# The first batch's V loaded in runs of three keys and ordered by TensorE, with w_in behind it in one go

## The chip, the cores and the metric

The kernel runs on one core of a Trainium2 chip. A core has TensorE (PE) for matrix products, VectorE (DVE), ScalarE (ACT) and GpSimd (POOL) for work on rows, and SyncE (SP), which here issues the DMAs. PSUM is where TensorE writes; SBUF is where everything else lies. The metric is the device time of one execution in microseconds, taken as the median of several runs.

## The reference

Inputs are q, k and v of 8 batches, 8 heads, 576 positions and 64 values each, and two weights, w_in (512 x 2048) and w_out (2048 x 512), with two scalars s and b. What is computed:

```
scores = q @ k^T / 8, kept where |i - j| <= 32       (per batch and head)
attn   = softmax(scores) @ v
x      = attn, heads side by side: 4608 tokens x 512
h      = relu(x @ w_in)
out    = (s * h * h + b) @ w_out                      (4608 x 512, float32)
```

All inputs are float32; the kernel casts them to bf16 for the products.

## The kernel before, in words

The whole program is a list of tasks. A task has an engine, one or more instructions, an estimated cost, the buffers that it reads and writes, and a key that says how early it is wanted. A planner inside the program (`plan`) walks through the tasks with a model of engines and DMA queue and writes down an order for each engine; `emit` then puts waits on semaphores between the engines. A change of one task's cost or key can therefore move instructions anywhere, and on each engine the order is then fixed: an instruction that waits holds up all behind it.

Attention of a batch is cut into tiles of 64 positions (nine of them) and units of two tiles (five, the last with one tile). The first batch goes its own way at the start. q and k come in pairs of heads, `load_pair`, nine positions to a partition in runs of 2304 bytes; they are cast (line 592 or 593), turned by TensorE against an identity (line 599) into W, which is two PSUM banks, and copied out (lines 605 and 606). The scores of one head pair (line 832) go to SC or O, two more pairs of banks, and ScalarE takes the exponential (line 854).

V of a unit comes with one DMA (`load_v`, line 566): keys on partitions, heads and values side by side, so that each run in memory has the 64 values of one key and head, 256 bytes. It is cast to bf16 by GpSimd or VectorE (`cast_v`, line 575) straight into VB, where it stands with its keys in order. The attention products (line 747) read VB and the exponentials; unit u needs V of units u and u-1. They go to SC, O or AVN. VectorE divides by the row sums (lines 769 and 771), TensorE turns the result (line 778) and ScalarE copies it to XT (line 786).

The second part works on token blocks of 96, 128, 128, 160, 256, 256 and then 512 tokens. `s1` multiplies XT with w_in into one of the two W banks (line 980), ScalarE applies relu (987), VectorE squares (989) into GT. `s2` multiplies GT with w_out into O (998), and line 1014 scales and adds before the store. For the first four blocks the w_out product is split into `early` (line 1029), which follows the arrival of w_out. w_in and w_out come in eight pieces of 512 KB each through a ring of eight staging buffers (line 538) and are all cast by GpSimd (line 541); a piece is issued when GpSimd or another engine has freed its buffer. The column sums of w_out (line 1038) need all of w_out.

The order of SP's loads is fixed by rising keys: the eight pairs of q and k, then what `ORDER0` says, numbers below 8 for units of V and 8 to 11 for the four quarters of w_in:

```
ORDER0 = (0, 1, 8, 2, 3, 4, 9, 10, 11)
EV0 = ("pool", "dve", "pool", "dve", "pool")
```

then the two scalars, w_out, and q, k and V of the second batch. `EV0` names the engines that cast the units of V. GpSimd also makes the masks of the later batches (lines 470, 475, 505, 508), some of them between casts of weights.

Of the kernel before, what the change touches and what calls it, by code (L numbers as in the profile page):

```python
# [12 lines left out]
D = 64  # L13
# [11 lines left out]
LAG = 1  # L25
K0 = ("dve", "dve", "dve", "dve")
Q0 = ("act", "pool", "pool", "pool")
ORDER0 = (0, 1, 8, 2, 3, 4, 9, 10, 11)
WINE = ("pool", "pool", "pool", "pool")
FIRST = ((0, 0), (1, 0), (2, 0), (0, 1), (1, 1), (2, 1), (3, 0), (3, 1), (0, 2), (1, 2), (2, 2), (3, 2), (0, 3), (1, 3), (2, 3), (3, 3))  # L30
WOUTE = (("pool", "pool"),) * 4
# [9 lines left out]
CASTE = (("pool", "pool"), ("pool", "dve"))  # L41
SLACK = (1000.0, 2000.0, 3000.0, 3000.0)
PACEV = ((-1,-1,0,0,1),(0,0,1,1,2),(0,0,1,1,2))
EV0 = ("pool", "dve", "pool", "dve", "pool")
BANK1 = ("W", "SC", "SC", "AVN", "AVN")
EV1 = ("pool", "pool", "pool", "pool", "pool")
EV2 = ("dve",) * 5
# [269 lines left out]
def bass_sliding_window_symmetric__then__act_starrelu_kernel(  # L317
# [23 lines left out]
    with ExitStack() as es:  # L341
# [45 lines left out]
        ONESW = sb((128, 128), BF16, "onesw")  # L387
        IDENT = sb((128, 128), BF16, "ident")
        GT = [sb((128, 16, 512), BF16, "gt") for _ in range(2)]
        R1 = [sb((128, 512), BF16, "r1") for _ in range(NR1)]  # L390
        OUTS = [sb((128, DM), F32, "outs") for _ in range(NOUT)]
        CVEC = sb((128, DM), F32, "cvec")
# [134 lines left out]
        def load_weights(which, i, x, key, eng):  # L527

            si = take("stg", NSTG)
            stg = STG[si].rearrange("p (a c) -> p a c", a=2)  # L530
            if which == "in":
                src = moe_w_in.rearrange("(kc p) f -> p kc f", p=128)[:, 2 * x:2 * x + 2, i * 512:(i + 1) * 512]
                dst = WIN_BF[:, 2 * x:2 * x + 2, i * 512:(i + 1) * 512]
            else:
                f0 = 4 * i + 2 * x
                src = moe_w_out.rearrange("(fc p) c -> p fc c", p=128)[:, f0:f0 + 2, :]
                dst = WOUT_BF[:, f0:f0 + 2, :]
            add("sp", lambda e: e.dma_start(stg, src), 600.0, writes=[("STG", si)], key=key,
                dma=("l", 16, 100.0 if which == "in" else 85.0))
# [32 lines left out]
        def cast_v(c, u, key, eng, slack):  # L572
            vs, vb, n = number(c, u) % NUNIT, number(c, u) % (2 * NUNIT), 64 * len(tiles(c, u))
            add(eng, (lambda e: e.copy(VB[0:n, vb, :, 0:D], VST[0:n, vs, :, :])) if eng == "act" else
                (lambda e: e.tensor_copy(VB[0:n, vb, :, 0:D], VST[0:n, vs, :, :])),  # L575
                {"act": 617.0, "dve": 420.0, "pool": 750.0}[eng],
                reads=[("VST", vs)], writes=[("V", vb)], key=key, slack=slack)

        def load_pair(b, name, pr, load_key):

# [310 lines left out]
        def attention():  # L891
            seq = {"k": -200.0}

            def nxt():
                seq["k"] += 1.0
                return seq["k"]
# [5 lines left out]
            for pr in range(NPAIR):  # L902
# [425 lines left out]
```

## Time and profile before

| | us |
|---|---|
| median of three timed runs | 318.2 (317.32 to 319.56) |
| profiled execution | 316.02 |
| its span, first to last instruction | 314.2 |
| TensorE busy in the span | 297.0 (95%) |
| VectorE, ScalarE, GpSimd busy | 190.1, 140.8, 89.3 |
| mean granted TensorE clock | 0.989 |

The busy time of TensorE counts an instruction from its start to its modelled end; matmuls overlap. The granted clock is the share of full speed that the chip lets TensorE run at. DMA shares above 1 come from overlapping packets. A line of the chain of waits gives the start in us from the span's start, the length and what it was.

### The profile page before, as it was taken

How to read it: one execution, taken by the hardware profiler on the slowest of the kernel's cores; microseconds unless marked ns; L12 is line 12 of the kernel's file. 1: busy time of each engine (PE TensorE's matmuls, PEld its weight loads, DVE VectorE, ACT ScalarE, POOL GpSimd, SP SyncE). 2: the span in 40 equal slices, each digit the busy share in tenths (PEclk: the TensorE clock that was granted, in tenths of full speed). 3: DMA queues.
4: the chain of work that ended last, by engine and by line, in shares of the span. 5: the costliest groups of instructions: out<-in, count | busy, mean ns of one | idle time of the engine just before them, and what ended most of it. 6: DMA issues, size and time to landing. Idle time of an engine off the chain costs nothing.

```text
span 314.2 us, 8417 instructions
## 1 busy us (share of the span) xinstructions
PE 297.0 (95%) x3557; PEld 162.3 (52%) x3602; DVE 190.1 (61%) x377; ACT 140.8 (45%) x219; POOL 89.3 (28%) x109
## 2 busy tenths in 40 slices
PE   7698999899999999999999999999999999999995
PEld 3477855477644554544444444444444444444444
DVE  3455594875796796887578477856555543333312
ACT  4736435266635775653266335444444333333300
POOL 3468864635136136132313421260000000000000
PEclk9969999999999999999999999999999999999999
DMA  7999999998998998798999799997111110100122
GB/s 261 296 303 392 388 286 282 191 172 263 254 166 210 288 160 163 237 228 140 219 297 165 161 190 336 166 157 176 52 52 50 52 46 33 37 35 33 37 96 74
DMA packets 98985, 56.13 MB, mean 179 GB/s; under 512 B 74048, under 2 KB 88128, under 8 KB 98944
## 3 DMA queue, kind: packets, MB, share of 16 engines
q1 hardware_dynamic: 98944, 55.56, 74.8%
q8 instruction: 29, 0.48, 0.7%
q14 instruction: 12, 0.10, 0.1%
HBM read 36.70 MB, written 9.44 MB: 147 GB/s over the span
## 4 chain that ended last, share of the span: by engine, by line
PE 79%; DMA 9%; DVE 4%; issue 3%; POOL 2%; ACT 2%; SPq 1%; POOLq 0%
PE w L980 34%; PE o L998 32%; DMA stg<-in_k_dram 4%; PE avn L747 3%; DMA stg<-in_moe_w_in_dram 3%; DMA vst<-in_v_dram 2%; PE o L1029 2%; PE avn L1029 2%; DVE gt L989 2%; PE sc L689 2%; PE w L599 1%; ACT r L987 1%; PE avn L778 1%; POOL win L541 1%; DVE outs L1014 1%
## 5 line engine op out<-in xcount | busy, mean ns | idle before, releaser
L980 PE MATMUL w<-xt,win 128*128 128x512 bf16 (+4 forms) x813 | 141.3, 315 | 3.6 <-issue 1.9
L987 ACT ACTIVATE r<-w 128x512 bf16<-128x512 f32 (+2 forms) x148 | 86.6, 586 | 107.2 <-PE w L980 88.8
L998 PE MATMUL o<-wout,gt 128*128 128x512 bf16 (+1 forms) x510 | 123.1, 372 | 2.0 <-issue 1.4
L989 DVE TENSOR_TENSOR gt<-r 128x512 bf16<-128x512 bf16 (+2 forms) x148 | 75.0, 511 | 79.3 <-ACT r L987 78.7
L980 PEld LDWEIGHTS w<-xt,win 128*128 128x128 bf16 x832 | 70.2, 99 | 53.8 <-issue 0.8
L998 PEld LDWEIGHTS o<-wout,gt 128*128 128x128 bf16 x528 | 50.5, 98 | 54.6
L638 POOL CAST nat<-stg 128x1024 bf16<-128x1024 f32 (+1 forms) x21 | 24.6, 1174 | 62.1 <-DMA stg<-in_q_dram 41.3
L655 POOL COPY kt<-ktr 128x512 bf16<-128x512 bf16 (+1 forms) x30 | 30.8, 1027 | 38.4 <-DMA ktr<-nat 36.9
L717 ACT ACTIVATE ex<-sc 128x1024 bf16<-128x1024 f32 (+1 forms) x29 | 29.7, 1023 | 22.2 <-PE avn L747 21.3
L1014 DVE SCALAR_TENSOR_TENSOR outs<-o,sb,cvec 128x512 f32<-128x512 f32 (+1 forms) x35 | 25.4, 729 | 13.6 <-PE o L998 13.5
L721 DVE TENSOR_TENSOR ex<-ex,mask 128x1024 bf16<-128x1024 bf16 (+1 forms) x29 | 23.0, 794 | 1.6 <-ACT ex L717 0.6
L771 DVE TENSOR_TENSOR xn<-avn,rec 128x512 bf16<-128x512 f32 (+1 forms) x31 | 21.4, 690 | 0.9
L747 PE MATMUL avn<-vb,ex 64*64 64x65 bf16 x952 | 20.1, 199 | 0.6 <-issue 0.3
L747 PEld LDWEIGHTS avn<-vb,ex 64*64 64x64 bf16 x952 | 13.1, 108 | 13.8 <-issue 7.6
L638 DVE CAST nat<-stg 128x1024 bf16<-128x1024 f32 (+1 forms) x15 | 12.7, 849 | 2.3 <-DMA stg<-in_q_dram 1.3
L575 DVE CAST vb<-vst 128x512 bf16<-128x512 f32 (+1 forms) x30 | 13.0, 439 | 1.4 <-DMA vst<-in_v_dram 1.4
L689 PE MATMUL sc<-qt,kt 64*64 64x128 bf16 x440 | 11.7, 216 | 0.0
L769 DVE RECIPROCAL rec<-avn 128x8 f32<-128x8 f32 (+1 forms) x31 | 6.3, 203 | 6.9 <-PE avn L747 6.6
L786 ACT COPY xt<-avn 128x512 bf16<-128x512 bf16 (+2 forms) x14 | 7.2, 523 | 6.2 <-PE avn L778 6.2
L1029 PE MATMUL o<-wout,gt 128*128 128x512 bf16 x29 | 8.2, 379 | 1.0 <-POOL mask L508 0.8
L541 POOL CAST win<-stg 128x1024 bf16<-128x1024 f32 x8 | 8.4, 1048 | 1.8 <-DMA stg<-in_moe_w_in_dram 1.4
L1029 PE MATMUL avn<-wout,gt 128*128 128x512 bf16 x27 | 8.1, 380 | 0.7 <-issue 0.6
(90 smaller groups left out, 137.7 us busy)
## 6 DMA issues: line engine op xcount, KB each, us to landing
out_dram<-outs SPq DMA_DIRECT2D x35, 256.0 KB, 2.6
vst<-in_v_dram SPq DMA_DIRECT2D x32, 256.0 KB, 5.9
stg<-in_q_dram SPq DMA_DIRECT2D x6, 1024.0 KB, 6.8
stg<-in_k_dram SPq DMA_DIRECT2D x6, 1024.0 KB, 10.4
stg<-in_moe_w_in_dram SPq DMA_DIRECT2D x8, 512.0 KB, 6.4
stg<-in_moe_w_out_dram SPq DMA_DIRECT2D x8, 512.0 KB, 10.0
stg<-in_q_dram SPq DMA_DIRECT2D x8, 288.0 KB, 4.9
stg<-in_k_dram SPq DMA_DIRECT2D x8, 288.0 KB, 4.8
```

The lines of the kernel that those rows point to most:

```text
L638: add(eng, lambda e, x=x: e.tensor_copy(nat[0:top, 1024 * x:1024 * x + 1024].rearrange("p (i h d) -> p h i d", h=H, i=2), stg[0:top, :].re ...
L655: add("pool", lambda e, c=c, w=w: e.tensor_copy(KT[slot][:, :, c:c + w].rearrange("p a (s i) -> p a s i", i=4), KTR[slot][:, :, :, c // 4: ...
L717: add("act", lambda e, dst=flat_dst, src=flat_src: e.activation(dst, src, AF.Exp, bias=0.0, scale=0.125), 190 + 0.833 * 512 * len(hs), rea ...
L721: add("dve", lambda e, flat=flat, mask=mask: e.tensor_tensor(flat, flat, mask, ALU.mult), 130 + 0.53 * 512 * len(hs), reads=[("E", ei, hp, ...
L747: return [lambda e: e.matmul(av[64 * x:64 * x + 64, h, 0:D + 1], lhsT=buf[64 * g:64 * g + 64, h % 2, h // 2, c:c + 64], rhs=VB[64 * g:64 * ...
L771: add("dve", lambda e: e.tensor_tensor(XN[xi][0:p1, :].rearrange("p (a c) -> p a c", a=H), av[0:p1, :, 0:D], REC[ri][0:p1, :].rearrange("p ...
L980: add("pe", [lambda e, g=g, kc=kc: e.matmul(wt[:, g, :], lhsT=WIN_BF[:, kc, (f0 + g) * 128:(f0 + g + 1) * 128], rhs=XT[:, kc, t0 % XR:t0 % ...
L987: add("act", lambda e: e.activation(rt, wt, AF.Relu, bias=0.0, scale=1.0), 190 + 0.833 * ng * nt, reads=[("W", wb)], writes=[("R1", rb)], ...
L989: add("dve", lambda e: e.tensor_tensor(GT[gs][:, f0:f0 + ng, g0:g0 + nt], rt, rt, ALU.mult), 130 + 0.53 * ng * nt, reads=[("R1", rb)], wri ...
L998: add("pe", [lambda e, fc=fc: e.matmul(O[:, ob, 0:cn], lhsT=GT[gs][:, fc, g0:g0 + 128], rhs=WOUT_BF[:, fc, c0:c0 + cn], start=(fc == 0), s ...
L1014: add("dve", lambda e: e.scalar_tensor_tensor(OUTS[us][:, 0:cn], bank, SB128[:, 0:1], CVEC[:, c0:c0 + cn], ALU.mult, ALU.add), 200 + 1.07 ...
L1029: add("pe", [lambda e, fc=fc, bank=bank, gs=gs, g0=g0: e.matmul(bank, lhsT=GT[gs][:, fc, g0:g0 + 128], rhs=WOUT_BF[:, fc, :], start=(fc == ...
```

## The change

V of the first batch is loaded in three groups of three tiles (192 keys). A partition gets three keys in a row of one head, 768 bytes in one run; 64 partitions hold one head and 64 the other, and four DMAs make a group, one per pair of heads. The staged group is cast to bf16 into VN, which lies in a part of GT's second buffer that is not in use yet. Key 3p + i of a group then stands on partition p at place i, so the keys are not in order on partitions. For each unit TensorE multiplies with a slice of PICK, a matrix of zeros and ones made from the identity: for each i of three it takes the columns that send partition p to row 3p + i of the wanted tiles, and the three products add up in PSUM. The result is V in order, in W or SC, and VectorE or ScalarE copies it to VB.

The eight pieces of w_in follow after the three groups without V between them; before, the first two stood between the second and third unit of V. The planner's cost of a w_in piece on the DMA queue is 86 instead of 100. The loads of the second batch's V wait for the casts of the groups, since they share a staging buffer.

```diff
-ORDER0 = (0, 1, 8, 2, 3, 4, 9, 10, 11)
+RUN = 3
+V0 = ("pool", "pool", "dve")
+BANK0 = ("W", "SC", "W", "W", "W")
...
-EV0 = ("pool", "dve", "pool", "dve", "pool")
+EV0 = ("dve", "dve", "dve", "act", "act")
...
+        VN = GT[1][:, 0:6, :].rearrange("p (s x) c -> p s (x c)", x=2)[:, :, 0:RUN * 256].rearrange(
+            "p s (a i d) -> p s a i d", a=NPAIR, i=RUN)
+        PICK = GT[1][:, 6, 0:65 * RUN]
...
-                dma=("l", 16, 100.0 if which == "in" else 85.0))
+                dma=("l", 16, 86.0 if which == "in" else 85.0))
...
+        def load_rows(s, load_key):
+
+            dst = VST.rearrange("p u h d -> p (u h d)")[:, 256 * RUN * s:256 * RUN * (s + 1)].rearrange(
+                "p (a c) -> p a c", a=NPAIR)
+            k0 = 64 * RUN * s
+            add("sp", [lambda e, pr=pr: e.dma_start(
+                dst[:, pr, :], v[0, 2 * pr:2 * pr + 2, k0:k0 + 64 * RUN, :].rearrange("h (p i) d -> h p (i d)", i=RUN))
+                for pr in range(NPAIR)], 480.0 * NPAIR, writes=[("VS", s)], key=load_key, dma=("l", 32, 38.0))
+
+        def cast_rows(s, eng):
+
+            src = VST.rearrange("p u h d -> p (u h d)")[:, 256 * RUN * s:256 * RUN * (s + 1)]
+            add(eng, lambda e: e.tensor_copy(VN[:, s, :, :, :].rearrange("p a i d -> p (a i d)"), src),
+                {"dve": 520.0, "pool": 900.0}[eng], reads=[("VS", s)],
+                writes=gt_res(1, 2 * s, 0, 512) + gt_res(1, 2 * s + 1, 0, 512), key=-32.0 + s, slack=200.0)
+            land["rows", s] = g.tasks[-1]
+
+        def pick():
+
+            grid = PICK.rearrange("p (a r) -> p a r", r=RUN)
+            add("dve", lambda e: e.memset(PICK, 0.0), 150, writes=gt_res(1, 6, 0, 512), key=-57.0)
+            add("dve", [lambda e, p0=p0: e.tensor_copy(grid[p0:p0 + 64, 0:64, RUN - 1], IDENT[p0:p0 + 64, p0:p0 + 64])
+                        for p0 in (0, 64)], 250, reads=["IDENT"], writes=gt_res(1, 6, 0, 512), key=-57.0)
+
+        def place_v(u, eng):
+
+            name = BANK0[u]
+            bank, res, ts = {"W": W, "SC": SC}[name], [(name, 0), (name, 1)], tiles(0, u)
+            n = 64 * len(ts)
+            if ts[0] // RUN == ts[-1] // RUN:
+                jobs = [(0, n, ts[0])]
+            else:
+                jobs = [(64 * x, 64, t) for x, t in enumerate(ts)]
+            add("pe", [lambda e, i=i, hp=hp, p0=p0, m=m, t=t: e.matmul(
+                bank[p0:p0 + m, hp, 0:256].rearrange("p (a c) -> p a c", a=NPAIR),
+                lhsT=PICK[64 * hp:64 * hp + 64, RUN - 1 + 64 * (t % RUN) - i:RUN - 1 + 64 * (t % RUN) - i + m],
+                rhs=VN[64 * hp:64 * hp + 64, t // RUN, :, i, :], start=(i == 0), stop=(i == RUN - 1),
+                skip_group_check=True) for i in range(RUN) for p0, m, t in jobs for hp in (0, 1)], 450.0,
...
+            dst = VB[0:n, u, :, 0:D].rearrange("p (a i) c -> p i a c", i=2)
+            src = bank[0:n, :, 0:256].rearrange("p i (a c) -> p i a c", a=NPAIR)
+            add(eng, (lambda e: e.copy(dst, src)) if eng == "act" else (lambda e: e.tensor_copy(dst, src)),
+                {"act": 620.0, "dve": 600.0}[eng], reads=res, writes=[("V", u)], key=-26.5 + u)
...
-            for t in ORDER0:
-                if t < 8:
-                    load_v(0, t, nxt(), "sp")
-                    cast_v(0, t, -28.0 + t, EV0[t], 300.0)
-                else:
-                    w("in", t - 8)
+            pick()
+            for s in range(NTILE // RUN):
+                load_rows(s, nxt())
+                cast_rows(s, V0[s])
+            for i in range(4):
+                w("in", i)
+            for u in range(NUNIT):
+                place_v(u, EV0[u])
...
-                    load_v(1, step[1], nxt(), "sp")
+                    load_v(1, step[1], nxt(), "sp", [land["rows", s] for s in range(NTILE // RUN)])
```

The planner then puts the placing of units 0 to 2 on TensorE right behind the scores and ahead of the first attention product, unit 3 behind the second product and unit 4 behind the third; the first w_in product, which before stood behind the second attention product, now stands behind the fourth.

More of the change, by code (lines that the diff above doesn't have):

```diff
@@ new lines, in place_v @@
+        def place_v(u, eng):
[11 more added lines that the diff above has]
+                skip_group_check=True) for i in range(RUN) for p0, m, t in jobs for hp in (0, 1)], 450.0,
+                reads=[r for s in sorted({t // RUN for t in ts}) for r in gt_res(1, 2 * s, 0, 512) + gt_res(1, 2 * s + 1, 0, 512)] +
+                gt_res(1, 6, 0, 512), writes=res, key=-26.5 + u, slack=300.0)
+            dst = VB[0:n, u, :, 0:D].rearrange("p (a i) c -> p i a c", i=2)
+            src = bank[0:n, :, 0:256].rearrange("p i (a c) -> p i a c", a=NPAIR)
+            add(eng, (lambda e: e.copy(dst, src)) if eng == "act" else (lambda e: e.tensor_copy(dst, src)),
+                {"act": 620.0, "dve": 600.0}[eng], reads=res, writes=[("V", u)], key=-26.5 + u)
```

## The prediction

> **What bounds the kernel now.** I read the page's 40 slices first, then the windows, then what TensorE waited for, then the chain.
>
> ```profile
> PE   7698999899999999999999999999999999999995
> PEclk9969999999999999999999999999999999999999
> DMA  7999999998998998798999799997111110100122
> ```
>
> A slice is 7.86 us. TensorE is full almost to the end; what it lost lies in the first eight slices, and there the DMA engines are full too. The third slice (15.7 to 23.6 us) has a granted clock of 0.6. The next table cuts that region into stretches of 3.41 us, chosen because the clock falls at 14.79 and returns at 21.61, and then at 41.30 (column sums of w_out) and 62.30 (early w_out sums done).
>
> ```profile
> core 0: us, PE busy (x) PEld busy (x) DVE busy (x) ACT busy (x) POOL busy (x), PEclk, DMA share, GB/s
> 7.97:11.38 3.41, 2.85 (x94) 1.73 (x98) 1.94 (x4) 2.51 (x4) 1.24 (x3) 1.00 1.19 281
> 11.38:14.79 3.41, 1.61 (x74) 1.06 (x66) 1.09 (x2) 2.00 (x4) 1.19 (x3) 1.00 1.05 315
> 14.79:18.20 3.41, 2.91 (x63) 2.26 (x58) 1.78 (x4) 2.07 (x4) 2.50 (x4) 0.50 1.15 214
> 18.20:21.61 3.41, 3.26 (x84) 2.77 (x83) 2.49 (x6) 0.49 (x1) 1.72 (x3) 0.50 0.97 344
> 21.61:41.30 19.69, 17.93 (x277) 15.29 (x278) 10.74 (x22) 10.59 (x22) 17.22 (x26) 1.00 1.04 385
> 41.30:62.30 21.00, 19.18 (x416) 10.79 (x422) 15.56 (x28) 7.99 (x12) 11.36 (x14) 1.00 1.08 246
> ```
>
> The second number after the stretch is TensorE's busy time. From 21.61 us on it is work that bounds: idle is 1.76 us of 19.69 and 1.82 us of 21.00. So faster loading can return at most those 3.6 us there, though w_in and w_out are still arriving. Before 21.61 TensorE idles 1.80 us in the stretch with busy 1.61 and, at half clock, does 6.17 us of busy time that would take about half, some 3.1 us lost. What stands in line there:
>
> ```profile
> 10.24 6.61 DMA vst<-in_v_dram
> 18.54 8.66 DMA stg<-in_moe_w_in_dram
> 31.80 0.38 PE o L1029
> ```
>
> These are three lines of the chain of waits (start, length). V units 2 to 4 are landing until 16.85 us and later, w_in until 27.20 us, and the first w_out product starts at 31.80, after TensorE sat idle 0.76 us for a GpSimd task behind the casts:
>
> ```profile
> PE o L1029 <- POOL mask L508: 0.8, 1, 0.8
> PE sc L747 <- ACT xt L786: 0.7, 1, 0.7
> ```
>
> These are the only two waits of TensorE on other engines above 0.5 us between 22 and 62 us.
>
> **Loads.** Removed: five V DMAs of 256-byte runs (4608 runs). Added: twelve of 768-byte runs (1536 runs), the same 1.18 MB. In the stretch 10 to 11 us only such V moved, at 229 GB/s; q and k (2304-byte runs) moved at 366 GB/s from 3 to 9 us, weights at 383 from 19 to 27. No row has 768 bytes: the bounds are 219 GB/s (the stretch 14.2 to 18.6 us) and 383, that is 5.4 and 3.1 us for all V. From 229 and 383 a fixed part per run can be estimated (256 B x 16 engines / 229 GB/s = 17.9 ns, 2048 B = 85.6 ns, so 8.2 ns plus 0.0378 ns per byte): 37 ns per run, 332 GB/s, 3.55 us. I take that. The last k landed at 9.9 us, so the three groups land at about 11.1, 12.3 and 13.45, where units 2, 3 and 4 of before were cast at 16.98, 18.27 and 18.92. SP issues the twelve from 4.57 us at 0.46 each (its q and k issues), done at 10.1, ahead of the data. Then w_in comes unbroken: 4.19 MB at 383 GB/s is 10.95 us, and with the landing it is there at about 24.4, not 27.2. GpSimd (1.04 us per weight cast, 17.22 busy of 19.69 us here) gets the last w_in cast done near 25.6 instead of 30.06 and the last w_out cast near 37 instead of 41.27.
>
> **The new path of V.** A cast of a group is 128x768: between GpSimd's 0.62 (512 wide) and 1.04 us (1024), so 0.83; VectorE 0.64 (0.42 and 0.85). Done at 12.0, 13.1, 14.1. VectorE's third cast stands in its queue ahead of the first PSUM copy, so that copy can't start before 14.1. The 0/1 matmuls: 36 of 256 columns. A 512-column product steps by 0.216 us, so 0.108 each; alone that is 3.9 us, but the two halves use different partitions, and the scores of line 832 do that too: 16 of 128 columns take 0.42 with their tail, about a third of their sum. I take pairs, 0.35 per unit, 1.7 in all at full clock, twice that at half. The five copies out of PSUM: between VectorE's cast of 0.42 and its 0.76 for the 576-wide copy of line 606; 0.65, ScalarE 0.62 (its 0.59 to 0.64).
>
> Now the chain, with hops of 0.05 us as in the timeline, at the clocks of before. Scores end at 13.66 as before. Unit 0 is placed by 14.1 and copied 14.15 to 14.80; unit 1 copied to 15.48; unit 2 needs W back, is placed by 15.7, copied to 16.4. The first attention product needs unit 1 out of SC: it starts at 15.55, where before it started at 14.25. Unit 3 is placed behind the second product (17.75), copied by ScalarE to 18.4; the third product runs 18.0 to 18.95; unit 4 placed by 19.6, copied to 20.25. The fourth runs 19.85 to 20.8; the first w_in product, which needs W, starts at 21.0 instead of 17.33. After that the fifth product, a transpose and block 1 follow without a gap, and block 2's first w_in product starts at 23.65; before, 23.17. So attention starts 1.3 us later but loses its waits for V (1.40 us of VectorE, 1.33 of GpSimd), and the sum to this point is +0.5.
>
> From there to 62 us: the 0.76 us wait goes, since w_out's first cast is done near 27 and TensorE comes for it only near 29. What is late next is nothing on loads; TensorE's work is next. Of the 0.68 us wait on ScalarE and the copies ahead of the column sums I count 0.3 back. The order after 62 us changes in places, with the same instructions; I count 0, uncertain by 0.7 either way. GpSimd's and ScalarE's edits cost nothing else: GpSimd idles 1.36 and 2.09 us where its two casts stand, ScalarE 0.87 and 0.44 beside its two copies; without that cover each would cost its 0.6 to 0.8 us.
>
> **Sum:** +0.5 - 0.76 - 0.3 = -0.6 us. Against the profiled execution (316.02 us, span 314.2) that is 315.4; the three timed runs have a median of 318.2, 2.2 above it, and by them it is 317.6, my forecast.
>
> [...] In the rows, the clock fell after a stretch with busy 1.61 of 3.41 us, did not return after one with 2.91 and returned after one with 3.26. [...]
>
> **Rivals.** (1) Clock kept, waits filled: the added matmuls raise busy in 11.38 to 14.79 from 1.61 to some 2.2, and rows show that 2.85 keeps full clock and 1.61 doesn't. Then block 2 starts near 23.1 (-0.05 for +0.5), which gives -1.1; if earlier loads also free all of the 3.6 us of idle, of which 1.06 is counted, -3.6; with copies of 0.42 instead of 0.65, three in a row, -4.3. Against: VectorE's copies, not TensorE, set the chain. Middle -3.3, 314.9.
> (2) Slower: the half clock lasts. The place is 18.2 to 21.6 us, where TensorE waits for copies; another stretch of 3.41 us at half clock costs 1.7, two 3.4. With one it is +1.1, with two +2.8; and V's third group landing after 14.1 adds one for one, as VectorE stands behind it. Above 1% from a total of 3.8 over my sum, for example two stretches and a landing at 14.5. For it: the row with 2.91 busy that did not bring the clock back. Middle +3.4, 321.6.
> (3) The runs of three don't load faster: 219 GB/s puts the last group at 15.3, w_in at 26.2; the chain is 1.2 later, the rest stays: +0.6, 318.8.
>
> **Numbers.** Forecast 0.47 (316 to 319.5), clock kept 0.28, slower 0.17, no faster load 0.08. The range from 313.9 (-4.3) to 321.0 (+2.8, two stretches) leaves out the outer part of (2) and what neither bound covers. One per cent is 3.2 us, about what a measurement of this kernel can tell from no change. Faster than that 0.22, being most of (1); slower 0.15, most of (2); within it 0.63.
>
> **What would show it.** Groups of V cast at 11.1, 12.3 and 13.5; the first attention product at 15.5; w_in's last cast over by 26; the first w_in product near 21; no wait of the first w_out product; the granted clock low for two stretches of 3.41 us. I am wrong if it is low for none or for three and more, if the copies take well over 0.65 us, or if the order after 62 us opens waits that the rows of before don't have.

## The result, and the profile after

The changed kernel takes 337.77 us (median of five runs, 336.78 to 338.70); the kernel before takes 318.2 us. The ratio is 1.0612, with a 95% interval of 1.0574 to 1.0649. The forecast was 317.6 us and the range ended at 321.0, so the time lies outside both. The profiled execution took 337.77 us, with a span of 335.9 us against 314.2 before.

These are the same three lines of the page of the changed kernel. A slice is now 8.4 us.

```profile
PE   8501699998999999999999999999999999999996
PEclk9955589999999999999999999999999999999999
DMA  7113999899999979989979979997421110100012
```

TensorE is idle in the third slice and nearly so in the fourth (digits 0 and 1), where it was nearly full before (9 and 8). The DMA line, which stood at 9 there, stands at 1, 1 and 3 in slices two to four. The transfers did not become faster, they nearly stopped. The table of the same stretches says it in numbers (columns: start and end in us, length, busy time of each engine, granted clock, share of the 16 DMA engines, GB/s):

```profile
core 0: us, PE busy (x) PEld busy (x) DVE busy (x) ACT busy (x) POOL busy (x), PEclk, DMA share, GB/s
7.97:11.38 3.41, 3.06 (x104) 2.41 (x98) 1.49 (x3) 2.92 (x4) 0.96 (x2) 1.00 0.40 148
11.38:14.79 3.41, 2.16 (x82) 1.30 (x76) 1.52 (x2) 2.51 (x5) 0.00 (x0) 1.00 0.14 47
14.79:18.20 3.41, 0.00 (x0) 0.00 (x0) 0.00 (x0) 1.39 (x2) 0.45 (x1) 0.83 0.14 47
18.20:21.61 3.41, 0.82 (x6) 0.29 (x6) 0.00 (x0) 0.00 (x0) 0.38 (x1) 0.50 0.14 46
21.61:41.30 19.69, 5.57 (x122) 3.33 (x122) 4.42 (x10) 1.01 (x2) 5.42 (x7) 0.50 0.60 204
41.30:62.30 21.00, 20.47 (x378) 17.31 (x375) 13.96 (x27) 10.69 (x21) 17.62 (x28) 0.93 0.99 345
```

From 11.38 to 21.61 us the core moves 46 to 47 GB/s at a share of 0.14. A share of 0.14 of sixteen engines is 2.2 engines; with the share at 1 and the same rate per engine it would by my estimate be some 330 GB/s (46 / 0.14). By this reading the runs themselves are fast and only two engines carry them; the experiments test it. SP's own timeline shows what this holds up (start, length, line, count of issues), and the chain of waits goes through the same place:

```profile
4.56 23.79 SPq L589 DMA_DIRECT2D vst<-in_v_dram  x12
28.40 7.27 SPq L543 DMA_DIRECT2D stg<-in_moe_w_in_dram  x8
```

```profile
15.65 2.04 SPq L589
...
26.31 8.81 DMA vst<-in_v_dram
...
43.54 1.12 PE w L1032 x16
```

The first two issues of V take SP 0.70 and 0.82 us, the third 3.18, and seven of the other nine 2.04, instead of the 0.46 that I had taken from q and k: 96 KB in 2.04 us are 48 GB/s, about the rate at which V moves (46 to 47), so by these numbers SP gets rid of a transfer only as fast as the two engines drain it. w_in, whose first issue stood at 6.47 us before, is issued from 28.40. TensorE waits for the three groups one after another (longest wait first):

```profile
PE w L617 <- DVE vb L626: 8.4, 1, 8.4
PE sc L617 <- POOL gt L596: 7.7, 1, 7.7
PE w L617 <- POOL gt L596: 4.5, 1, 4.5
```

The first of the three names VectorE's copy, but VectorE stood behind its own cast of the third group, for which it waited 21.5 us. The groups were cast at 17.75, 26.18 and 35.15 us; the first attention product ran at 37.12, where it ran at 14.25 before. From 14.79 to 41.30 us TensorE's idle time is 20.1 us, against 2.4 before. These 17.7 us are most of the 21.7 us by which the span grew. The placing products, five times 0.82 to 0.85 us, would be about the rest; what the longer time at half clock cost, and what was regained later, was not separated.

### The profile page after: what moved, and what is told of

The parts are those of the page before. It is cut to its first block, busy times and chain, and to the rows that moved or that the text cites. A ratio compares the mean times of both kernels' runs of the same rounds, so it can differ in the third digit from the quotient of the medians.

```text
span 335.9 us, 8536 instructions
## 1 busy us (share of the span) xinstructions
PE 307.0 (91%) x3638; PEld 164.9 (49%) x3638; DVE 192.4 (57%) x382; ACT 142.2 (42%) x221; POOL 90.1 (27%) x108
## 4 chain that ended last, share of the span: by engine, by line
PE 83%; SPq 7%; POOL 4%; DMA 3%; issue 1%; DVE 0%; ACT 0%; POOLq 0%
PE w L1032 35%; PE o L1050 33%; SPq L589 6%; PE avn L797 4%; DMA vst<-in_v_dram 3%; POOL wout L546 3%; PE sc L739 2%; PE o L1081 2%; PE avn L1081 2%; SPq L633 1%; PE avn L828 1%; PE sc L797 1%; PE w L649 1%; POOL win L546 1%; PE w L617 1%
## 5 line engine op out<-in xcount | busy, mean ns | idle before, releaser
L1032 PE MATMUL w<-xt,win 128*128 128x512 bf16 (+4 forms) x832 | 144.3, 315 | 0.0
L1050 PE MATMUL o<-wout,gt 128*128 128x512 bf16 (+1 forms) x528 | 126.5, 373 | 0.0
L1041 DVE TENSOR_TENSOR gt<-r 128x512 bf16<-128x512 bf16 (+2 forms) x148 | 76.5, 522 | 77.8 <-ACT r L1039 77.1
L705 POOL COPY kt<-ktr 128x512 bf16<-128x512 bf16 (+1 forms) x30 | 32.5, 1085 | 43.9 <-DMA ktr<-nat 42.4
L688 POOL CAST nat<-stg 128x1024 bf16<-128x1024 f32 (+1 forms) x21 | 23.6, 1125 | 57.5 <-DMA stg<-in_q_dram 36.3
L771 DVE TENSOR_TENSOR ex<-ex,mask 128x1024 bf16<-128x1024 bf16 (+1 forms) x29 | 22.7, 783 | 1.7 <-ACT ex L767 0.5
L797 PE MATMUL avn<-vb,ex 64*64 64x65 bf16 x952 | 20.1, 199 | 0.3
L797 PEld LDWEIGHTS avn<-vb,ex 64*64 64x64 bf16 x952 | 13.1, 108 | 13.3 <-issue 7.8
L617 PE MATMUL w<-gt 64*128 64x256 bf16 (+1 forms) x24 | 3.3, 409 | 12.8 <-DVE vb L626 8.4
L596 DVE CAST gt<-vst 128x768 bf16<-128x768 f32 x1 | 0.6, 560 | 21.5 <-DMA vst<-in_v_dram 21.5
L626 ACT CAST vb<-w 128x512 bf16<-128x512 f32 (+1 forms) x2 | 1.2, 584 | 24.4 <-PE w L617 24.4
L546 POOL CAST win<-stg 128x1024 bf16<-128x1024 f32 x8 | 8.5, 1068 | 10.5 <-DMA stg<-in_moe_w_in_dram 10.4
L688 DVE CAST nat<-stg 128x1024 bf16<-128x1024 f32 (+1 forms) x15 | 11.0, 732 | 0.0
```

Source lines behind the costliest of these rows:

```text
L688: add(eng, lambda e, x=x: e.tensor_copy(nat[0:top, 1024 * x:1024 * x + 1024].rearrange("p (i h d) -> p h i d", h=H, i=2), stg[0:top, :].re ...
L705: add("pool", lambda e, c=c, w=w: e.tensor_copy(KT[slot][:, :, c:c + w].rearrange("p a (s i) -> p a s i", i=4), KTR[slot][:, :, :, c // 4: ...
L771: add("dve", lambda e, flat=flat, mask=mask: e.tensor_tensor(flat, flat, mask, ALU.mult), 130 + 0.53 * 512 * len(hs), reads=[("E", ei, hp, ...
L797: return [lambda e: e.matmul(av[64 * x:64 * x + 64, h, 0:D + 1], lhsT=buf[64 * g:64 * g + 64, h % 2, h // 2, c:c + 64], rhs=VB[64 * g:64 * ...
L1032: add("pe", [lambda e, g=g, kc=kc: e.matmul(wt[:, g, :], lhsT=WIN_BF[:, kc, (f0 + g) * 128:(f0 + g + 1) * 128], rhs=XT[:, kc, t0 % XR:t0 % ...
L1041: add("dve", lambda e: e.tensor_tensor(GT[gs][:, f0:f0 + ng, g0:g0 + nt], rt, rt, ALU.mult), 130 + 0.53 * ng * nt, reads=[("R1", rb)], wri ...
```

## The experiments

**How many engines.** V's piece for one issue is `v[0, 2 heads, 192 keys]` cut as head, partition, run: 2 x 64 x 192 values. Since 192 of 576 keys are taken, head and partition can't be merged into one dimension of 128, as they can for q and k, which take all 576. My reading, an estimate from the 2.2 engines above, was then that a transfer is dealt to the engines by its first dimension, and that has two entries here. Four kernels change the first dimension and keep the runs of 768 bytes; the first two change the number of DMAs with it, the last two don't. The first puts the keys first and makes one DMA of each half of the partitions, with four heads in it:

```diff
-            add("sp", [lambda e, pr=pr: e.dma_start(
-                dst[:, pr, :], v[0, 2 * pr:2 * pr + 2, k0:k0 + 64 * RUN, :].rearrange("h (p i) d -> h p (i d)", i=RUN))
-                for pr in range(NPAIR)], 480.0 * NPAIR, writes=[("VS", s)], key=load_key, dma=("l", 32, 38.0))
+            vp = v.rearrange("b (a two) s d -> b two a s d", two=2)
+            add("sp", [lambda e, hp=hp: e.dma_start(
+                dst[64 * hp:64 * hp + 64, :, :], vp[0, hp, :, k0:k0 + 64 * RUN, :].rearrange("a (p i) d -> p a (i d)", i=RUN))
+                for hp in (0, 1)], 480.0 * NPAIR, writes=[("VS", s)], key=load_key, dma=("l", 32, 38.0))
```

> The groups of V come with two DMAs each, one per half of the partitions, whose access begins with the 64 partitions and not with the two heads: six DMAs of 192 KB in place of twelve of 96 KB, the same 1536 runs of 768 bytes, the same order on all engines. In the changed kernel V moved at 46 GB/s with a DMA share of 0.14, close to 2 of 16 engines. Theory (the changed kernel's DMAs are dealt to two DMA engines because their first dimension has two entries): V moves on all 16, at about 330 GB/s, the last group is cast at about 13.5 us instead of 35.1, and the time is that of my prediction, 316 to 319 us. Rival F (each small DMA pays some 2.1 us, one after another): six of them take 12.6 us, the last group at 22 us, about 325 us. Rival L (runs of 768 bytes are slow in themselves): no change, 338 us.

The second leaves a DMA one head, so that only partitions remain in front:

```diff
-                dst[:, pr, :], v[0, 2 * pr:2 * pr + 2, k0:k0 + 64 * RUN, :].rearrange("h (p i) d -> h p (i d)", i=RUN))
-                for pr in range(NPAIR)], 480.0 * NPAIR, writes=[("VS", s)], key=load_key, dma=("l", 32, 38.0))
+                dst[64 * hp:64 * hp + 64, pr, :], v[0, 2 * pr + hp, k0:k0 + 64 * RUN, :].rearrange("(p i) d -> p (i d)", i=RUN))
+                for pr in range(NPAIR) for hp in (0, 1)], 480.0 * NPAIR, writes=[("VS", s)], key=load_key, dma=("l", 32, 38.0))
```

> Each DMA of V is halved, one head at a time: 24 DMAs of 48 KB, whose first dimension is the 64 partitions; the same 1536 runs of 768 bytes, the same order otherwise. Theory of two engines: all 16 work again, but SP needs 24 issues of 0.46 us from 4.6 us on, so the last group is there at 17 to 18 us and the time is 319 to 322 us. Rival F (2.1 us for each DMA): 24 take 50 us, the last group at about 60 us, 360 us or more. Rival L (slow runs): 338 us.

The third and fourth keep the order head, partition, run and the twelve DMAs of 96 KB, but take four heads of 96 keys and eight heads of 48 keys. The edit of the fourth:

```diff
-                dst[:, pr, :], v[0, 2 * pr:2 * pr + 2, k0:k0 + 64 * RUN, :].rearrange("h (p i) d -> h p (i d)", i=RUN))
+                dst[:, pr, :], v[0, 0:8, k0 + 48 * pr:k0 + 48 * pr + 48, :].rearrange("h (p i) d -> h p (i d)", i=RUN))
```

> Twelve DMAs of 96 KB in runs of 768 bytes as in the changed kernel, but each takes four heads of 32 partitions in place of two heads of 64. This puts the values of V on other partitions than the rest of the kernel expects, so the attention is that of a V in another order; no work is left out. Theory of two engines: the first dimension has four entries, so four DMA engines work, DMA share 0.25, 93 GB/s, the last group at about 22 us instead of 35.1, about 325 us. Rivals F and L: no change, 46 GB/s and 338 us.

> As the run with four heads, with eight heads of 16 partitions in each DMA; the values of V again stand in another order, and no work is left out. Theory of two engines: eight DMA engines work, DMA share 0.5, about 186 GB/s, the last group at about 15.6 us, 319 to 320 us. Rivals F and L: no change, 46 GB/s and 338 us.

| first dimension | DMAs | V, GB/s | DMA share | SP per issue (mean), us | groups cast at, us | time, us |
|---|---|---|---|---|---|---|
| 2 heads (the change) | 12 | 46 | 0.14 | 1.98 | 17.75, 26.18, 35.15 | 337.77 |
| 4 heads | 12 | 93 | 0.27 | 1.06 | 14.0, 18.2, 23.5 | 328.34 |
| 8 heads | 12 | 178 | 0.55 | 0.71 | 11.9, 15.2, 17.6 | 323.24 |
| 64 keys, 4 heads behind | 6 | 243 | 1.12 | 0.71 | 12.2, 14.2, 16.0 | 321.27 |
| 64 keys, 1 head | 24 | 81 | 0.33 | 0.69 | 12.0, 17.7, 22.7 | 327.27 |

The rates are those of the stretch from 10 to 13 us (10 to 14 for the change). The times with four heads, eight heads and one head are of one execution each, the other two are medians. Here are the packets of that stretch, of the change and then of four and of eight heads:

```profile
DMA packets 246, 0.19 MB, mean 46 GB/s; under 512 B 4, under 2 KB 246, under 8 KB 246
```

```profile
DMA packets 373, 0.28 MB, mean 93 GB/s; under 512 B 11, under 2 KB 373, under 8 KB 373
```

```profile
DMA packets 718, 0.53 MB, mean 178 GB/s; under 512 B 42, under 2 KB 717, under 8 KB 717
```

But for a few small ones the packets are the same 768 bytes; rate and share double with the first dimension, 22 to 23 GB/s for each of its entries. That settles the cause: with a fixed price for each DMA, or with runs that are slow in themselves, twelve DMAs of 96 KB in such runs would have stayed at 46 GB/s. The share says the same: 0.14, 0.27 and 0.55 of sixteen are 2.2, 4.3 and 8.8 engines, and with 64 keys in front and four heads behind them it is 1.12. What holds between 8 and 64 entries no run shows. The kernel with one head also has 64 keys in front and still a share of 0.33, but not a steady one: within the stretch it goes from 0 to 0.9 and more, and the rate from 0 to 256 GB/s. It has 24 issues at 0.69 us, and SP is its limit: 48 KB per 0.69 us are 71 GB/s, near the 81 in the table. Its time of 327.27 us missed what the theory had said, because I had counted the issues too cheaply. The rates with four and eight heads came as said, the times did not: 328.34 and 323.24 us for 325 and 319 to 320, with the last group 1.5 and 2 us later than said.

**What the change is worth with its transfers spread.** The kernel with the keys first was then timed against the kernel before: 321.27 us against 318.01 us, ratio 1.0068 (1.0034 to 1.0102), where 316 to 319 us was expected. So of the loss of some 19.6 us about 16.5 go with the two engines, and a small loss is left. Its groups still came later than I had predicted, at 243 GB/s with the DMA engines full. The next kernel writes all 128 partitions in each DMA: 64 keys first, then two heads on alternate partitions. The 0/1 matrices then pick every second partition; twelve DMAs as in the change.

```diff
-                dst[:, pr, :], v[0, 2 * pr:2 * pr + 2, k0:k0 + 64 * RUN, :].rearrange("h (p i) d -> h p (i d)", i=RUN))
+                dst[:, pr, :], v[0, 2 * pr:2 * pr + 2, k0:k0 + 64 * RUN, :].rearrange("two (p i) d -> p two (i d)", i=RUN))
...
-                lhsT=PICK[64 * hp:64 * hp + 64, RUN - 1 + 64 * (t % RUN) - i:RUN - 1 + 64 * (t % RUN) - i + m],
-                rhs=VN[64 * hp:64 * hp + 64, t // RUN, :, i, :], start=(i == 0), stop=(i == RUN - 1),
+                lhsT=PICKS[hp][:, RUN - 1 + 64 * (t % RUN) - i:RUN - 1 + 64 * (t % RUN) - i + m],
+                rhs=VN[:, t // RUN, :, i, :], start=(i == 0), stop=(i == RUN - 1),
```

> Twelve DMAs of 96 KB in runs of 768 bytes over 128 partitions, as in the changed kernel; only the order of the first two dimensions is turned, 64 keys of two heads instead of two heads of 64 keys, so heads lie on alternate partitions, and the matrix of zeros and ones is made for either head over all 128 partitions (the same number of products, which no longer run in pairs: 0.65 us a unit at full clock instead of 0.5). Theory (engines are dealt by the first dimension; and with 16 engines the run with the keys first was held at some 240 GB/s because each of its DMAs writes to only one half of the partitions): all 16 engines and both halves work, V is limited by SP's issues, 0.6 us each, from 4.6 to 11.9 us, the last group is cast at about 14 us instead of 15.96 there, and the time is 1 to 2 us below that run's 321.3: 319 to 320.5 us. Rival (768-byte runs on 16 engines move at 240 GB/s wherever they go): landing at 12.2, 14.2 and 16 us as there, 321 to 322 us. Rival F (2.1 us per DMA): 338 us.

It took 320.26 us against 317.82, ratio 1.0064 (1.0034 to 1.0095): in the expected range, but by the ratio no better than with the keys first. SP's timeline of this kernel shows why the last of the groups, cast at 11.09, 13.09 and 15.45 us, came only 0.5 us sooner than there and not at 14:

```profile
4.69 8.57 SPq L589 DMA_DIRECT2D vst<-in_v_dram  x12
13.31 4.57 SPq L543 DMA_DIRECT2D stg<-in_moe_w_in_dram  x8
```

(Its profiled execution took 323.81 us and lies above its median.) An issue costs SP 0.71 us here on average, and the DMA engines are only 0.62 busy from 10 to 13 us: the transfers wait for SP now.

**The other half of the change.** In the kernel before, `ORDER0` alone puts w_in behind all of V; V keeps its short runs.

```diff
-ORDER0 = (0, 1, 8, 2, 3, 4, 9, 10, 11)
+ORDER0 = (0, 1, 2, 3, 4, 8, 9, 10, 11)
```

> The kernel before, with one part of the change alone: all of w_in behind all five units of V, V still in 256-byte runs and without products to order it. Theory (the loads of V are on the path at the start, w_in is early enough): V units 2 to 4 are cast some 3 us earlier (w_in's first two pieces, 1 MB at 383 GB/s, no longer stand ahead of them), the attention products of units 2 to 4 come earlier, w_in's last cast stays near 30 us; 316 to 318 us, no slower than before. Rival (the first w_in products were what kept TensorE busy and its clock up between 17 and 23 us): w_in's first quarter comes 3 us later, the clock is low for one stretch of 3.41 us more, 319 to 321 us.

318.06 us against 317.82, ratio 1.0004 (0.9969 to 1.0038): no effect that could be told. In its profiled execution (320.16 us) the last three units were cast at 14.29, 15.4 and 15.74 us, some 3 us earlier as expected, but w_in came later, the first w_in product moved from 17.33 to 21.86, and TensorE waited for other work instead (2.2 us for VectorE's division ahead of a transpose, none above 0.4 before).

**A halt that no wait explains.** In both repaired kernels TensorE stood still inside the third attention product, and the profile names nothing that it waited for. These are lines of TensorE's timeline, of the kernel with keys first and of the one with keys and then heads (start, length, line, tile, shape, count, idle time before it):

```profile
23.32 0.27 PE L798 MATMUL avn<-vb,ex 64*64 64x65 bf16 x5 [1.61 <-issue]
```

```profile
23.87 0.27 PE L798 MATMUL avn<-vb,ex 64*64 64x65 bf16 x5 [3.60 <-issue]
```

Counted from the start of TensorE's program, both come after 348 matmuls. In the kernel before, halts of 0.68 and 0.63 us come after 221 and 476. All the distances are 127 or 128. From these distances alone I took them for the places where TensorE's program goes on to its next block, which has to be fetched; if so, other products ahead of them move them. Two kernels, made from the one with keys and then heads, replace the five warm-up products by 104 and by 24 small ones:

```diff
-        add("pe", [lambda e: e.matmul(W[:, 1, :].rearrange("p (a c) -> p a c", a=4), lhsT=ONESW[:, :], rhs=ones,
-                                       start=True, stop=True)] * WARM,
+        add("pe", [lambda e, i=i: e.matmul(W[64 * (i % 2):64 * (i % 2) + 64, 1, 0:64], lhsT=ONESW[64 * (i % 2):64 * (i % 2) + 64, 0:64],
+                                            rhs=ONESW[64 * (i % 2):64 * (i % 2) + 64, 0:64], start=True, stop=True) for i in range(104)],
```

> Starts from the kernel with the keys first on all 128 partitions (320.26 us), in whose trace TensorE stood still for 3.60 us in the middle of the third attention product, waiting for nothing that the profile names; in every trace so far such halts came after the 221st, 348th or 476th matmul of TensorE's program, which are 127 or 128 apart. Here the five warm-up products of 128x512 at the start are replaced by 104 of 64x64, which compute nothing that is used either; every later product is the same and comes 99 matmuls later in the count. Theory I (the halts belong to the count: the next piece of TensorE's program is brought over DMA engines that are full of loads): the halt after 348 matmuls now falls ahead of or in the placing of the third unit, where TensorE waits for VectorE's copy anyway (1.75 us), so the third attention product runs without a halt above 0.5 us, and the time is 316.5 to 318.5. Rival (the halt belongs to the place: something the third attention product needs comes late): a halt of 1.5 to 3.6 us stays in the third attention product, and the time stays at 319.5 to 321.

> The same with 24 small products in place of the five, so that every later product comes 19 matmuls later in the count. Theory I: the halt stays inside the third attention product but moves forward, from after 27 of its 32 matmuls to after 8 or so; the time is 319 to 322. Rival (the place): it stays after 27 of the 32.

With 104 the third attention product ran without a halt. Two halts stand elsewhere in TensorE's timeline, after 476 and 603 matmuls; the third line, of its waits, is what the gain turned into:

```profile
22.46 0.59 PE L798 MATMUL sc<-vb,ex 64*64 64x65 bf16 x18 [1.03 <-issue]
28.98 1.44 PE L1033 MATMUL w<-xt,win 128*128 128x128 bf16 x23 [0.80 <-issue]
```

```profile
PE o L1082 <- POOL wout L546: 1.5, 1, 1.5
```

With 24 the halt that theory I placed after 348 did not appear at all, and one of 0.68 us stands after 476. So the halts keep to the count and not to the product, as theory I had it, but a place in the count can pass without a halt.

The traces say more than that. From 5 to 66 us all of them together hold 22 such halts of 0.3 us or more, and each comes after 221, 348, 476, 603, 985 or 1112 matmuls, to within one where no record is missing. An instruction queue, which the page lists beside the loads' queue, moved a packet of 16 KB ahead of every one of them, and TensorE went on 1.3 to 1.9 us after that packet had ended: the halt of 3.60 us ended at 23.87, its packet had run from 21.40 to 22.41. Such packets are some 4 us and more apart, so 22 times out of 22 is hardly chance, and it speaks for a fetch. What sets the length, 0.3 to 3.6 us, stays open, since no record tells when a packet was asked for.

The time did not fall: 320.05 us against 317.89 with 104, ratio 1.0069 (1.0029 to 1.0108), where 316.5 to 318.5 was expected; the one execution with 24 took 321.28, inside its 319 to 322. The granted clock stayed at 1.00 up to 31.4 and 33.2 us and TensorE ran ahead, to stand 1.5 and 3.5 us for the first cast of w_out.

**Loads with two issuing engines.** If SP's issuing is what keeps V slow in these kernels, a second issuer should free it. In the kernel with 104 small warm-up products ScalarE takes the second group's four DMAs.

```diff
-            add("sp", [lambda e, pr=pr: e.dma_start(
-                dst[:, pr, :], v[0, 2 * pr:2 * pr + 2, k0:k0 + 64 * RUN, :].rearrange("two (p i) d -> p two (i d)", i=RUN))
-                for pr in range(NPAIR)], 480.0 * NPAIR, writes=[("VS", s)], key=load_key, dma=("l", 32, 38.0))
+            for x in (0, 1):
+                act = s == 1
+                add("act" if act else "sp", [lambda e, pr=pr: e.dma_start(
+                    dst[:, pr, :], v[0, 2 * pr:2 * pr + 2, k0:k0 + 64 * RUN, :].rearrange("two (p i) d -> p two (i d)", i=RUN))
+                    for pr in (2 * x, 2 * x + 1)], 600.0 * 2, writes=[("VS", s, x)], key=-59.0 if act else load_key + 0.5 * x,
+                    dma=("l", 16, 38.0), waits=[issue_after[x]] if act else [])
```

> Starts from the kernel with 104 small warm-up products (320.05 us), where V still came slowly: SP needed 8.77 us to issue the twelve DMAs of V, the DMA engines were only 0.55 busy from 11.38 to 14.79 us, the last group was cast at 15.22 and the first piece of w_in at 17.88. Here ScalarE issues the four DMAs of the second group, two at about 6.2 us and two at about 9, and SP the other eight. Theory S (SP's issuing is what is left of the slow V): SP is through with V by about 10.6 us, the DMA engines stay full from 10 to 14 us, the last group is cast at 13.7 to 14.3 and the first piece of w_in at about 16.5; TensorE's wait of 1.5 us for the first cast of w_out is gone, the granted clock stays up, and the time is 316.5 to 318.7. Rival (the transfers themselves are slow, or what bounds comes later than w_out's first piece): the last group stays at 14.8 to 15.2 us, or comes earlier with no effect, and the time is 319.5 to 320.5.

The last group was cast at 14.03 us and the first piece of w_in at 16.39, as theory S had it, and from 10 to 11 us V moved at 321 GB/s with the DMA engines full. These are the stretches of this kernel that answer to the third, fourth and, in part, fifth row shown of before:

```profile
14.79:18.20 3.41, 3.17 (x81) 2.32 (x78) 3.11 (x8) 1.15 (x2) 2.28 (x4) 1.00 1.02 352
18.20:21.61 3.41, 3.16 (x89) 2.33 (x87) 1.80 (x5) 2.03 (x4) 1.60 (x3) 1.00 0.99 353
...
28.40:31.80 3.40, 1.65 (x16) 1.01 (x14) 1.96 (x2) 0.83 (x2) 3.13 (x5) 1.00 1.06 388
```

The clock is full throughout, where before had two stretches at 0.50. Yet the time is 318.34 us against 316.93, ratio 1.0027 (0.9996 to 1.0058): inside the expected range for the time, but no gain, and the wait that was to go is there:

```profile
PE o L1091 <- POOL wout L546: 1.8, 1, 1.8
```

The last row above shows it as 1.65 us busy of 3.40 with the DMA engines full at 388 GB/s. GpSimd begins the first cast of w_out at 29.27 us, 1.21 earlier than before; TensorE starts its first w_out product at 30.37, 1.43 earlier than before, but has only 96 w_in products behind it and not 144. Eight of the missing ones step by 0.55 us (160 columns), so 48 are 3.3 us, and it is about 1.9 us behind in work. At the third attention product of the second batch, a place that both have with the same work behind it, it starts at 63.11 us against 61.57: 1.5 us behind.

**Where the pace comes from.** Two variants of the kernel before: the halts moved by 104 small warm-up products, and TensorE kept busy ahead of the first attention product by 24 of them, in the hope of holding the clock. The warm-up edit is the one shown above, with 80 products in the second, which has also this:

```diff
+            add("pe", [lambda e, i=i: e.matmul(W[64 * (i % 2):64 * (i % 2) + 64, 1, 0:64], lhsT=ONESW[64 * (i % 2):64 * (i % 2) + 64, 0:64],
+                                  rhs=ONESW[64 * (i % 2):64 * (i % 2) + 64, 0:64], start=True, stop=True) for i in range(24)],
+                500.0, reads=["ONESW"], writes=[("W", 0), ("W", 1)], key=-26.5)
             first_units()
```

> The kernel before, with 104 warm-up products of 64x64 in place of five of 128x512 and nothing else, so that the halts after 221 and 476 matmuls (0.68 and 0.63 us in its trace) fall on other products. Theory (they cost nothing there, since loads set the pace to 32 us): 317.3 to 318.5, the halt in the last scores is gone. Rival (each halt is paid in full): 316.5 to 316.8, 1.3 us less.

> The kernel before with 80 small warm-up products, and 24 more of the same kind, whose results are not used, ahead of the first attention product, where TensorE idles in the stretch with 1.61 us busy of 3.41 after which the granted clock was 0.5 for two stretches. Theory L (loads and their casts set the pace to 32 us): the clock stays up, TensorE comes to the first w_out product some 3 us earlier than 31.80 but waits for the first cast of w_out until about 31.5, and the time is 316.5 to 318. Rival (the 3.1 us that the half clock costs come back whole): 314.5 to 315.5. If the clock falls all the same, 317.5 to 318.5 and neither is told.

The first: 317.38 us against 316.93, ratio 1.002 (0.9989 to 1.005). Both halts are gone, and TensorE waits 1.9 us for w_out's first cast where it waited 0.76 before:

```profile
PE o L1029 <- POOL wout L541: 1.9, 1, 1.9
```

So the halts were free in the kernel before; loads and their casts set the pace there up to 32 us. The second was inconclusive and slower, 320.62 us, ratio 1.0104 (1.0068 to 1.014), outside all three of its ranges. In its profiled execution (323.17 us) a halt of 1.59 us fell into the first attention product, after the 349th matmul, and the clock fell all the same (0.50 from 18.20 to 21.61 us). Whether a kept clock would come back as time in that kernel is not told.

```profile
16.92 0.25 PE L747 MATMUL sc<-vb,ex 64*64 64x65 bf16 x5 [1.59 <-issue]
```

The last run asks whether the order is at fault: the planner believed in early weights and put w_out ahead of w_in work that was ready. Made from the kernel with two issuing engines:

```diff
-                dma=("l", 16, 86.0 if which == "in" else 85.0))
+                dma=("l", 16, 100.0 if which == "in" else 95.0))
```

> The same as the kernel whose V is issued from two engines (318.34 us), with the planner's costs of a weight piece on the DMA queue 100 for w_in and 95 for w_out in place of 86 and 85. That alone changes orders: TensorE has 120 w_in products ahead of its first w_out product, 24 more than before this edit (144 stood there in the kernel before), about 1.7 us of work at 0.55 us per eight; in the trace of the two-engine kernel TensorE stood 1.75 us ahead of that product, waiting for the first cast of w_out. Theory (loads set the pace to 32 us, and the order written down for loads that come earlier left TensorE without work there): the wait goes below 0.4 us, and the time falls by 1 to 2 us, to 316.3 to 317.4. Rival (the work moved is only missing later, or another wait opens): 318 or more.

The wait for w_out is gone, as expected, and the time is 318.59 us against 317.82, ratio 1.0029 (0.9997 to 1.006): the rival's number, where 316.3 to 317.4 was expected. In the profiled execution other losses stand in its place, among them a halt after 476 matmuls and a second group that was cast at 15.05 us:

```profile
PE sc L623 <- POOL gt L601: 1.5, 1, 1.5
PE sc L803 <- issue: 1.4, 1, 1.4
```

No version of the idea was faster than the kernel before.

## Why the prediction was wrong

**The failed step is "Loads", the sum of V's rate.** "I take that", 332 GB/s and groups at 11.1, 12.3 and 13.45 us, became 46 GB/s and casts at 17.75, 26.18 and 35.15 us. The figure had been worked out from rows of V and weights by the length of a run. Those rows have DMA shares of 1.32 (229 GB/s), 1.10 (219) and 1.04 (383), so I take it that all sixteen engines were at work in them, and I did not ask over how many the new transfer would be dealt. The reading of run lengths itself was right: with 64 keys in front and issues from two engines V moved at 321 and, in the last run, 312 GB/s (from 10 to 11 us, DMA shares of 1.02 and 0.97). The bounds of the rate, 219 and 383, came from such rows too and so shared the fault. One of the rows was also misread: from 10 to 11 us not only V moved, 30 of the 638 packets are of weights and one is of 16 KB. From 10.0 to 10.5, where 418 of 422 packets are shorter than 512 bytes, as V's are, the rate is 228 GB/s, so the figure of 229 stands.

**SP's issues** were the second error in that step. 0.46 us is the price of q's and k's. With eight heads or 64 keys in front an issue of V cost 0.69 to 0.71 us on average, whether its access had two dimensions or three; what sets the price no run separated. Twelve of them are 8.5 us and end at 13.3, not 10.1. In the change itself, at 1.98 us an issue, this did not show.

**The new path of V** held but for the placing. In the kernel with the keys first, casts took 0.83 us on GpSimd and 0.56 on VectorE (said: 0.83, 0.64), copies 0.68 on VectorE and 0.59 on ScalarE (0.65, 0.62), and placing a unit 0.50 us at full clock and 0.82 at half (0.35 and twice that). With 128 rows in each product, as in the two-issuer kernel, it is 0.83 at full clock (0.65 expected).

**The chain** held where V came nearly as I had it. In the two-issuer kernel, with the last group at 14.03, attention began at 16.30 (said: 15.55) and w_in's products at 21.42 (21.0). That they came so near is partly luck: the sum had two stretches at half clock, and this kernel had none but paid 0.83 us for each placing. In the changed kernel it was rival 2's price that ruled: V's third group late "adds one for one". It was cast 21.7 us later than predicted (35.15 for 13.45), and the first attention product came 21.6 us later (37.12 for 15.55). That the span, too, grew by 21.7 us is in part chance, since the placing ran at half clock and some of TensorE's later idle time went. The mechanism was on the list, its size was not: the worst case that I wrote out had the group land at 14.5. (14.1, from which I counted that delay, is where its cast should be done; the landing was 13.45.) Rival 3 asked the right question, whether the runs load faster, and answered it with the slowest row at a full DMA share (219 GB/s at 1.10).

**What was to be gained** was not there either. The wait of the first w_out product, counted as -0.76, was 1.75 us in the two-issuer kernel and went only where TensorE itself came later, as in the last run. I had put w_in's last cast at 25.6 us. In that kernel it is over at 28.8, against 30.06 before, for the first piece is cast only at 16.39 and the masks stand between the last ones. The best form of the change, the two-issuer kernel, gives a ratio of 1.0027, by its interval -0.1 to +1.8 us of 317, so my -0.6 was too low even with the transfers spread. The terms -0.3 for other waits and 0 after 62 us could not be read apart from the rest. I had also read "from 21.61 us on it is work that bounds" from idle times. The variant of before with its halts moved shows that TensorE and w_out arrive there together. And some of that idle time was none: five gaps of up to 0.2 us at line 1029, 0.8 of the 1.82 us of the stretch 41.30 to 62.30, are most likely missing records, since that line shows 56 products in the trace of before and the same line 64 in the one with the keys first.

**The clock.** In the changed kernel it is at half from 17.0 to 44.4 us, where I had called myself wrong from three stretches of 3.41 us on. But my stretches were laid by the clock of the kernel before. In all traces each spell at half clock that ends within the program lasts a whole number of 3.41 us, from one to eight of them, and it begins at another time in each kernel: at 14.78 us before, at 15.78 in the kernel with the keys first. These are that kernel's stretches along its own steps:

```profile
15.78:19.19 3.41, 1.86 (x50) 1.13 (x51) 2.70 (x6) 0.39 (x1) 1.83 (x3) 0.50 1.06 389
19.19:22.61 3.42, 2.45 (x53) 1.44 (x54) 1.46 (x3) 1.01 (x2) 2.53 (x4) 0.50 1.05 386
22.61:26.02 3.41, 2.62 (x52) 1.79 (x52) 1.18 (x4) 1.12 (x2) 1.97 (x2) 0.50 1.05 386
26.02:29.43 3.41, 3.34 (x54) 3.00 (x53) 1.86 (x4) 1.59 (x3) 0.89 (x2) 0.50 1.05 387
```

The clock came back after the one with 3.34 us busy. Over such stretches of all traces up to 45 us it came back after 2.91 to 3.42 us busy and stayed at half after up to 3.28; it was lost after 0.47 to 2.25 and kept after 1.76 and more. So busy time goes with it, but no single value divides the cases. Transposes went with a kept clock too: in the two-issuer kernel the stretch from 5.11 to 8.53 us has 2.05 of its 2.72 us busy in transposes and the clock stayed, while before lost it after the stretch from 11.37 with 1.61, of which 0.21 are transposes.

## What to carry to other kernels

A rate read from a profile belongs to a transfer of a certain shape: before using it for a new access, write the access down as the DMA carries it and ask over how many engines it will be dealt (here 2, 4 and 8 entries in the first dimension moved 46, 93 and 178 GB/s). A DMA share far below one while the issues grow long is the sign that it is dealt to few (0.14 and 2.04 us in the change); slow issuing alone gives a low share too (0.33 with 24 DMAs at 0.69 us). Where loads and compute arrive at the same place together, as at this kernel's first w_out product, speeding up one side uncovers the other, and the order written for faster loads has to be tested with the loads that one really gets.

## What the runs showed of the hardware

- Half the partitions at a time went with a lower rate. With 768-byte packets and DMA shares of 1.12 and 0.97, transfers into 64 partitions moved 240 GB/s, transfers into 128 moved 312; the two kernels also differ in the size of a DMA and in the number of issuing engines, which was not separated. These are the packets from 10 to 11 us of the kernel with the keys first, and of the last run:

```profile
DMA packets 334, 0.24 MB, mean 240 GB/s; under 512 B 22, under 2 KB 334, under 8 KB 334
```

```profile
DMA packets 457, 0.31 MB, mean 312 GB/s; under 512 B 51, under 2 KB 457, under 8 KB 457
```

- With two, four and eight heads in front 22 to 23 GB/s moved for each of them (46 / 2, 93 / 4, 178 / 8); with 64 keys in front it was 19.5 for each of sixteen engines (312 / 16), or 15 into 64 partitions (240 / 16).
- From one issue to the next SP needed 0.47 us for loads of q or k and on average 0.69 to 0.73 for those of V with 768-byte runs where SP issued all of them and eight heads or 64 keys stood in front, at 48, 96 and 192 KB alike; most single ones took 0.43 and 0.60 to 0.63 us.
- TensorE halted after 221, 348, 476, 603, 985 and 1112 matmuls, from nothing to 3.6 us, at places in the program that an unrelated edit moves, and went on 1.3 to 1.9 us after a 16 KB packet of the instruction queue had ended.
- The spells at half clock that ended within the program lasted 3.41, 6.83, 10.24, 13.65, 17.07, 20.48 or 27.31 us, all multiples of 3.41.
